# The start of a fused attention and two-MLP kernel: ramp and first tile written out as one list of operations and loads

## The chip, the cores and the metric

One core of a Trainium2 chip. The metric is the device time of one execution in microseconds, the median of three runs of the kernel.

## The reference, cut to what matters

```
# attention: q, k, v are (4 batches, 8 heads, 576, 64), f32
scores = q @ k^T / 8;  masked: heads 0-3 keep the last 32 keys,
                       heads 4-7 every 4th of the last 128 keys
attn = softmax(scores); x = attn @ v       # -> (2304 tokens, 512)
# first MLP:   h = x @ w_in (512 x 2048); x = (h * sigmoid(h)) @ w_out
# second MLP:  x = ((x @ w1) * (x @ w2)) @ w3 @ w_out2    -> (2304, 512)
```

## The kernel before

**Units of the attention.** A unit is three blocks of 64 queries of one pair of heads in one batch: 48 units, 12 for each batch. A unit goes through a chain of operations, each named by a letter that the schedule tables use. S: scores on TensorE (6 products of 64x96 into PSUM, L203, tiles `s`). M: mask, row maximum and copy to SBUF on VectorE (L218, tile `sm`). E: exponential and row sum on ScalarE (L228). N: sum to reciprocal on VectorE (L236, L238, tile `rs`), then the product with it on GpSimd (L239). T: transposition of the weights on TensorE (L246, tiles `t`). W: copy of it from PSUM to SBUF, tile `at`, on VectorE for batch 0 (L253) and on ScalarE after it (L255). V: product with the values on TensorE (L266, tiles `o`). O: the result in two parts into `xT`, high on ScalarE (L276), low on VectorE (L277).

**Precision by two parts.** Each f32 operand of the MLPs is split into a high part and a low part, and each product is three matmuls. The weights come from memory as 64-bit words and are converted by a chain in `Convert`: `rebias` on ScalarE (L398), `bits` in two passes on VectorE (L406, L408), `high` on ScalarE (L417), `low` on VectorE (L423). Four buffers (`rawp`) hold raw weights. The chain for w_in's block f is called i0, i1, ..., that for w_out's u0, u1, ...

**The first MLP** runs over five chunks of tokens (`CH1`: 512, 512, 256, 512, 512) and sixteen blocks f of hidden columns; one pair (chunk, block) is a slot. Slot (c, f) issues, in the order that a string in `SLOT` gives, the twelve matmuls of `h` for the next block (L686), the twelve matmuls of `x` for its own block (L720, tiles `x2`), the tanh of the next block (`t` in the string: L702 on ScalarE, L703 on VectorE), its split (`g`: L465 on ScalarE, L466 on VectorE), steps of the conversion (`m`, `c`) in chunk 0, and steps of the attention of later batches (`a`). The attention of batch b has to be in `xT` when a chunk wants its tokens.

**The ramp.** Before the first slot the twelve units of batch 0 have to be through. The kernel before makes it in rounds: round n issues the steps of the string `ATT0`, each operation with a lag (S0 of unit n, M1 of unit n-1, and so on), and takes units 12 and 13 along as far as T. Rounds 8 to 16 also take a micro-step of the conversion (`START`), and after rounds 14 and 15 the first nine matmuls of h for blocks 0 and 1 (`AHEAD`). Then come the rest of h for block 0, its tanh and split, and the slot (0, 0).

**Order and memory.** All instructions are issued in the order in which the program is written; each engine and each DMA queue takes its own in that order and waits for semaphores. Queries and keys of batch 0 lie in the first 1152 columns of `stage4` to `stage7`, its values in those of `stage0` to `stage3`; these tiles are 2048 columns wide and become the weight tiles wf8 to wf15 after the ramp. The attention's PSUM tiles of batch 0 come from `ps_x` (4 banks, S and T) and `ps_a` (2 banks, V). Every DMA of the inputs goes over SyncE's queue, except one of the first.

Of the kernel before, what the change touches and what calls it, by code (L numbers as in the profile page):

```python
# [68 lines left out]
def tile_kernel(  # L69
# [83 lines left out]
    def load_qk(i):  # L153
        if i < NPAIR:
            t = stage[NPAIR + i][:, :2 * S].rearrange("p (x s) -> p x s", x=2)
        else:
            t = qkp.tile([P, 2, S], F32, tag="qk", name=f"qk_{i}")
        qk[i] = t
        if i == 0:
            first = NB * QB  # L160
            nc.sync.dma_start(out=t[:, 0, :first], in_=qT_d[i][:, :first])
            nc.scalar.dma_start(out=t[:, 1, :first], in_=kT_d[i][:, :first])
            nc.sync.dma_start(out=t[:, 1, first:], in_=kT_d[i][:, first:])
            nc.sync.dma_start(out=t[:, 0, first:], in_=qT_d[i][:, first:])
        else:
            nc.sync.dma_start(out=t[:, 0], in_=qT_d[i])
            nc.sync.dma_start(out=t[:, 1], in_=kT_d[i])
# [23 lines left out]
    def a_scores(n):  # L191
        b, p, u = unit(n)
        t = qk[n // NU]
        if n < RAMP:
# [16 lines left out]
    def a_max(n):  # L211
# [3 lines left out]
        sm = smp.tile([P, NB, KB], F32, tag="sm", name=f"sm_{n}")  # L215
# [18 lines left out]
    def a_norm(n):  # L234
        sm, su = st[n]["sm"], st[n].pop("su")
        nc.vector.tensor_scalar_add(su[:, :NB], su[:, :NB], 1e-9)  # L236
        rs = stp.tile([P, 4, 1], F32, tag="rs", name=f"rs_{n}")
        nc.vector.reciprocal(rs[:, :NB, 0], su[:, :NB])  # L238
        nc.gpsimd.tensor_tensor(sm, sm, rs[:, :NB].to_broadcast([P, NB, KB]), op=ALU.mult)  # L239

# [8 lines left out]
    def a_evac(n):  # L249
        t_v = st[n].pop("t")  # L250
        at = atp.tile([KB, NB, P], F32, tag="at", name=f"at_{n}")
        if n < PER_B:
            nc.vector.tensor_copy(at, t_v)  # L253
        else:
            nc.scalar.activation(at, t_v, AF.Copy)  # L255
        st[n]["at"] = at
# [15 lines left out]
    def a_out(n):  # L272
        b, p, u = unit(n)
        o_v = st.pop(n)["o"]
        def put(dst, src):
            nc.scalar.activation(dst[:, 0], src, AF.Copy)  # L276
            nc.vector.tensor_sub(dst[:, 1], src, f32(dst[:, 0]))  # L277
# [38 lines left out]
    def attention_steps():  # L316

        steps, rounds, begun = [], [], {op: 0 for op in A_OPS}
        chain = "SMENTWVO"
        after = dict(zip(chain[1:], chain))  # L320
        ramp = [(n, ATT0, RAMP) for n in range(PER_B + 5)]
        for n, order, units in ramp + [(n, ATT, NUNIT) for n in range(RAMP, NUNIT + 4)]:
            for x in order.split("|"):
                step = []
                for op, lag in zip(x[::2], x[1::2]):
                    ready = begun[after[op]] if op in after else NUNIT
                    while begun[op] < min(n - int(lag) + 1, units, ready):
                        step.append((op, begun[op]))
                        begun[op] += 1
                if step:  # L330
                    steps.append(step)
                    rounds.append(n)
        return steps, rounds

    class Stream:
        def __init__(self):
            (self.steps, self.rounds), self.at, self.out = attention_steps(), 0, 0
# [33 lines left out]
    class Convert:  # L371


        def __init__(self):
            self.todo = []
            self.nb = self.nh = self.nl = 0
            self.gate = 1 << 30
# [22 lines left out]
        def bits(self, i, x):  # L400
# [6 lines left out]
            else:  # L407
# [4 lines left out]
                self.load(i + 2)  # L412
# [261 lines left out]
    hps, h_done, gt, xps = {}, {}, {}, {}  # L674

    def h_begin(c, f):
        if (c, f) not in hps:
            hps[c, f] = ps_h.tile([P, 512], F32, tag="h", name=f"h_{c}_{f}")
            h_done[c, f] = 0

    def h_kt(c, f, kt):
# [8 lines left out]
        h_done[c, f] += 1  # L690

    def h_part(c, f, half):
        h_begin(c, f)
        for kt in range(h_done[c, f], 2 * half + 2):
            h_kt(c, f, kt)

    def g_ops(c, f):

        n = CH1[c][1]
        ps = hps.pop((c, f))[:, :n]  # L700
        t = gp.tile([P, 512], F32, tag="t", name=f"t_{c}_{f}", bufs=1)[:, :n]
        nc.scalar.activation(t, ps, AF.Tanh, scale=0.5)  # L702
        nc.vector.scalar_tensor_tensor(t, t, 1.0, ps, op0=ALU.add, op1=ALU.mult)  # L703
        gt[c, f] = t

    def g_split(c, f):
        n = CH1[c][1]
        t = gt[c, f]
        g = gp.tile([P, 2, 512], F32R, tag="g", name=f"g_{c}_{f}")[:, :, :n]
        split(g, t)  # L710
        gt[c, f] = g

    def x2_part(c, f, half):
# [3 lines left out]
        g = gt[c, f] if half == 0 else gt.pop((c, f))  # L717
        todo = [(m, sa, 0) for m in range(KT) for sa in (0, 1)] + [(m, 0, 1) for m in range(KT)]
# [206 lines left out]
    with tc.manual_schedule():  # L925
        nc.vector.memset(mask, 0.0)
        for i in range(2):
            load_qk(i)
# [3 lines left out]
        load_v0(0)  # L932
        load_qk(2)
        cv.load(0)
        load_v0(1)
        load_qk(3)
        cv.load(1)
        load_v0(2)
        load_qk(NPAIR)
        load_v0(3)  # L940
        load_qk(NPAIR + 1)

        k = 0
        while att.out < PER_B:
            n = att.rounds[att.at]
            att.step()
            k += 1
            end = att.rounds[att.at] != n
            if (k == 4 and START.get(n, 0) > 1) or (end and n in START):
                cv.micro()  # L950
            if end:
                k = 0
                if n in AHEAD:
                    f = AHEAD[n]
                    cv.need(IN[f])
                    h_begin(0, f)
                    for kt in range(KT - 1):
                        h_kt(0, f, kt)
        assert att.out == PER_B
# [3 lines left out]
        h_part(0, 0, 1)  # L963
# [200 lines left out]
```

## Time and profile before

| | |
|---|---|
| median of 3 runs | 831.85 us (831.84 to 832.21) |
| the profiled execution's own time | 828.14 us |
| its span, first to last instruction | 826.4 us |
| TensorE matmuls busy | 806.7 us, 98% |
| VectorE, ScalarE, GpSimd busy | 483.1, 322.6, 56.4 us |
| chain that ended last, by engine | PE 79%, DVE 8%, ACT 5%, issue 3%, DMA 2%, POOL 1% |

The profiled execution is one of several, and its time lies 3.7 us under the median of the other runs; sums of durations are made against it. PE is TensorE, DVE VectorE, ACT ScalarE, POOL GpSimd, SP SyncE's queue. A busy TensorE is not a TensorE at its peak: ends of matmuls are modelled, and the distance from one start to the next says more. `s`, `t` and `o` rows of PE count two records for each product in part (x12 for six f32 products).

### The profile page before, as it was taken

Reading aid. Unit: us, or ns where it says so; the run is one execution under the profiler, and the core shown is the slowest. Engines: PE = TensorE matmul, PEld = TensorE weight load, DVE = VectorE, ACT = ScalarE, POOL = GpSimd, SP = SyncE. Lnnn points to the kernel's source line nnn. Section 1 sums busy time; section 2 is a strip of 40 time slices with the busy share of each in tenths; the row PEclk is TensorE's granted clock in tenths of the full one; section 3 lists DMA queues with packets and bytes.
Section 4 is the critical chain, followed back from the end, with each engine's and each line's share of the span. In section 5 each row is a group of like instructions: output and inputs, shape, how many; then the busy total and the mean of one; then the engine's idle time right before and its main releaser. Section 6 shows DMA issues by size and latency. Waiting matters only on the chain.

```text
span 826.4 us, 12870 instructions
## 1 busy us (share of the span) xinstructions
PE 806.7 (98%) x4848; PEld 686.2 (83%) x4848; DVE 483.1 (58%) x1179; ACT 322.6 (39%) x819; POOL 56.4 (7%) x90
## 2 busy tenths in 40 slices
PE   7889999999999999999999999999999999999997
PEld 5667777777788999888878887888889999999996
DVE  5877778333324443222358877768888554774544
ACT  5766766444324453222344545433423211221112
POOL 3201110000000110000000000012210000000000
PEclk9999999999999999999999999999999999999999
DMA  9855663211111202000087544535640752035202
GB/s 261 231 178 181 194 184 114 66 51 52 52 36 48 77 9 63 14 1 1 0 289 263 200 152 146 160 102 215 238 172 1 248 188 75 1 140 204 90 1 76
DMA packets 43454, 98.61 MB, mean 119 GB/s; under 512 B 3968, under 2 KB 21888, under 8 KB 41344
## 3 DMA queue, kind: packets, MB, share of 16 engines
q1 hardware_dynamic: 42784, 96.91, 35.6%
q10 hardware_dynamic: 608, 0.89, 0.4%
q8 instruction: 38, 0.62, 0.3%
q14 instruction: 24, 0.20, 0.1%
HBM read 73.66 MB, written 24.12 MB: 118 GB/s over the span
## 4 chain that ended last, share of the span: by engine, by line
PE 79%; DVE 8%; ACT 5%; issue 3%; DMA 2%; POOL 1%; SPq 0%; ACTq 0%; POOLq 0%; DVEq 0%
PE x L720 20%; PE h L686 19%; PE bank L840 19%; PE o L891 10%; PE wp L663 4%; PE o L266 2%; PE o L203 2%; ACT sm L228 2%; PE t L246 2%; DVE g L466 1%; DVE wf L423 1%; ACT raw_u L398 1%; DVE sm L218 1%; ACT t L702 1%; PE s L203 1%
## 5 line engine op out<-in xcount | busy, mean ns | idle before, releaser
L686 PE MATMUL h<-xT,wf 128*128 128x512 f32 (+1 forms) x960 | 220.2, 374 | 0.0
L720 PE MATMUL x<-g,wf 128*128 128x512 f32 (+1 forms) x960 | 215.7, 371 | 1.7 <-ACT g L465 1.7
L720 PEld LDWEIGHTS x<-g,wf 128*128 128x128 f32 x960 | 166.8, 188 | 33.0 <-ACT g L465 3.1
L686 PEld LDWEIGHTS h<-xT,wf 128*128 128x128 f32 x960 | 165.2, 188 | 32.0 <-ACT xT L276 0.2
L840 PE MATMUL bank<-xT,wf 128*128 128x384 f32 x864 | 164.5, 336 | 0.7 <-ACT s L858 0.4
L840 PEld LDWEIGHTS bank<-xT,wf 128*128 128x128 f32 x864 | 151.4, 188 | 9.0 <-ACT s L858 1.4
L703 DVE SCALAR_TENSOR_TENSOR t<-t,h 128x512 f32<-128x512 f32 (+1 forms) x80 | 50.6, 632 | 132.3 <-ACT t L702 132.2
L891 PE MATMUL o<-wf,wf 128*128 128x512 f32 x432 | 110.7, 393 | 0.0
L702 ACT ACTIVATE t<-h 128x512 f32<-128x512 f32 (+1 forms) x80 | 44.0, 551 | 120.2 <-PE h L686 118.8
L891 PEld LDWEIGHTS o<-wf,wf 128*128 128x128 f32 x432 | 80.1, 188 | 12.8
L466 DVE TENSOR_TENSOR g<-t,g 128x512 fp32r<-128x512 f32 (+1 forms) x80 | 58.1, 727 | 53.8 <-ACT g L465 53.0
L465 ACT ACTIVATE g<-t 128x512 fp32r<-128x512 f32 (+1 forms) x80 | 46.8, 585 | 43.5 <-DVE t L703 43.5
L876 ACT ACTIVATE wf<-c 128x384 fp32r<-128x384 f32 x48 | 25.2, 526 | 86.7 <-DVE c L874 86.5
L239 POOL TENSOR_TENSOR sm<-sm,rs 128x288 f32<-128x288 f32 x48 | 36.1, 752 | 267.5 <-DVE rs L238 212.2
L228 ACT ACTIVATE sm<-sm,nm 128x96 f32<-128x96 f32 x144 | 52.0, 367 | 5.6 <-DVE nm L218 5.6
L858 ACT ACTIVATE s<-bank 128x384 f32<-128x384 f32 x24 | 11.8, 490 | 95.3 <-PE bank L840 84.7
L663 PE MATMUL wp<-wf,wf 128*128 128x512 f32 x192 | 46.9, 392 | 0.3 <-DVE wf L579 0.3
L276 ACT ACTIVATE xT<-o 128x192 fp32r<-128x192 f32 (+6 forms) x58 | 17.6, 303 | 74.2 <-DVE nm L218 63.9
L663 PEld LDWEIGHTS wp<-wf,wf 128*128 128x128 f32 x192 | 35.7, 188 | 7.4 <-DVE wf L579 0.7
L865 DVE TENSOR_TENSOR c<-u,bank 128x384 f32<-128x384 f32 x36 | 19.9, 552 | 31.9 <-PE bank L840 31.7
L575 ACT ACTIVATE wf<-y 128x512 fp32r<-128x512 f32 (+1 forms) x40 | 22.7, 584 | 28.5 <-DVE y L536 13.5
L246 PE MATMUL t<-ident,sm 128*96 128x128 f32 x144 | 25.7, 289 | 6.0 <-POOL sm L239 6.0
(84 smaller groups left out, 764.0 us busy)
## 6 DMA issues: line engine op xcount, KB each, us to landing
rawj<-in_w_dram SPq DMA_DIRECT2D x32, 512.0 KB, 3.8
raw_i<-in_w_in_dram SPq DMA_DIRECT2D x16, 512.0 KB, 3.9
raw_u<-in_w_out_dram SPq DMA_DIRECT2D x16, 512.0 KB, 3.5
setd<-wf SPq DMA_DIRECT2D x8, 1024.0 KB, 3.9
wf<-setd SPq DMA_DIRECT2D x8, 1024.0 KB, 5.2
setd<-wf SPq DMA_DIRECT2D x8, 768.0 KB, 5.8
wf<-setd SPq DMA_DIRECT2D x8, 768.0 KB, 6.8
xb<-x2d SPq DMA_DIRECT2D x12, 384.0 KB, 7.9
```

Of the source, the lines that this page charges most:

```text
L228: nc.scalar.activation(sm[:, j], sm[:, j], AF.Exp, bias=nm[:, j:j + 1], scale=-1.0, accum_out=su[:, j:j + 1],)
L239: nc.gpsimd.tensor_tensor(sm, sm, rs[:, :NB].to_broadcast([P, NB, KB]), op=ALU.mult)
L246: nc.tensor.transpose(t_ps[:KB, j], sm[:, j], ident)
L465: nc.scalar.activation(dst[:, 0], src, AF.Copy)
L466: nc.vector.tensor_sub(dst[:, 1], src, f32(dst[:, 0]))
L663: nc.tensor.matmul(wp_ps[i], a[:, i // 2, sa, i % 2 * P:(i % 2 + 1) * P], o[:, sb], start=(jt == 0 and x == 0), stop=(jt == NG - 1 and x = ...
L686: nc.tensor.matmul(ps, win(f, sa, kt), xT[:, kt, sb, r0:r0 + n], start=(kt == 0 and x == 0), stop=(kt == KT - 1 and x == 2),)
L702: nc.scalar.activation(t, ps, AF.Tanh, scale=0.5)
L703: nc.vector.scalar_tensor_tensor(t, t, 1.0, ps, op0=ALU.add, op1=ALU.mult)
L720: nc.tensor.matmul(xps[c][m][:, :n], wout(f, sa, m), g[:, sb], start=(f == 0 and sa == 0 and sb == 0), stop=(f == NF - 1 and sb == 1),)
L840: nc.tensor.matmul(b, a_op(s, a, sa, kt), b_op(x, sb, kt), start=(n == 0), stop=(n == 5),)
L891: nc.tensor.matmul(ops[pr][m], g_block(jj, n, sa)[:, m % 3 * P:(m % 3 + 1) * P], wp_v(f, sb), start=(first_ and x == 0), stop=(last and x ...
```

## The change

The ramp's rounds, `START`'s micro-steps, `AHEAD` and the first slot are replaced by one string, `START`, which lists every operation with its unit, and `FIRST`, which lists the loads in order. The letters are those above, with four splits: N becomes R (sum and reciprocal, VectorE) and N (product, GpSimd); O becomes H (high) and L (low); the copy after T is W (VectorE) or X (ScalarE), chosen for each unit; r, a, b, h, l are the conversion's five passes, p the matmuls of h by quarters, t u g e the tanh, its product, high and low split, x00 and x01 the halves of the first slot's `x`. Units 12 and 13 are no longer in it: the attention of batch 1 starts in slot (0, 1) with S of unit 12. Units 0 to 11 keep `sm` in columns 1152 to 1439 and `at` in columns 1440 to 1823 of the stage tile n mod 8, instead of in pools of three and two buffers. Queries and keys of units 12 to 17 are loaded inside the list (d4, d5). Raw weights are loaded four ahead, as soon as a buffer is free, instead of two ahead.

```
-ATT0 = "N3|W4|M1|V5S0L4|T3|E2|O5"
-RAMP = PER_B + 2
+START = (
+    "S0 M0 E0 S1 M1 E1 S2 R0 M2 N0 E2 R1 S3 N1 M3 S4 E3 R2 M4 T0 N2 S5 X0 R3 T1 "
...
+    "L6 W9 V8 H7 b0 T10 H8 X10 R11 h0 L7 N11 L8 V9 r1 l0 V10 H9 a1 T11 H10 L9 p00 X11 L10 "
...
+)
+FIRST = "q0a k0a k0b q0b q1 k1 v0 k2 q2 v1 i0 k3 q3 v2 i1 v3 u0 i2"
 ATT = "V3S1L3|M1T2O3|W2E1|N1"
-START = {8: 1, 9: 1, 10: 1, 11: 2, 12: 2, 13: 2, 14: 2, 15: 2, 16: 1}
-AHEAD = {14: 0, 15: 1}
...
-        sm = smp.tile([P, NB, KB], F32, tag="sm", name=f"sm_{n}")
+        if n < PER_B:
+
+            o = NU * NB * P
+            sm = stage[n % 8][:, o:o + NB * KB].rearrange("p (j k) -> p j k", j=NB)
+        else:
+            sm = smp.tile([P, NB, KB], F32, tag="sm", name=f"sm_{n}")
...
-    def a_evac(n):
+    def a_evac(n, act=True):
         t_v = st[n].pop("t")
-        at = atp.tile([KB, NB, P], F32, tag="at", name=f"at_{n}")
         if n < PER_B:
+            o = NU * NB * P + NB * KB
+            at = stage[n % 8][:KB, o:o + NB * P].rearrange("p (j k) -> p j k", j=NB)
+        else:
+            at = atp.tile([KB, NB, P], F32, tag="at", name=f"at_{n}")
+        if act:
+            nc.scalar.activation(at, t_v, AF.Copy)
+        else:
             nc.vector.tensor_copy(at, t_v)
...
-                self.load(i + 2)
+                self.load(self.ahead)
+                self.ahead += 1
...
+        BEGIN = {
+            "S": a_scores, "M": a_max, "E": a_exp, "R": a_sum, "N": a_mul, "T": a_transpose,
+            "W": lambda n: a_evac(n, False), "X": a_evac, "V": a_av, "H": a_high, "L": a_low,
+            "r": cv.rebias, "a": lambda i: cv.bits(i, 0), "b": lambda i: cv.bits(i, 1),
+            "h": cv.high, "l": cv.low, "d": load_qk, "t": lambda f: g_tanh(0, f), "u": lambda f: g_mul(0, f),
+            "g": lambda f: g_high(0, f), "e": lambda f: g_low(0, f),
+        }
+        for z in START.split():
+            op, z = z[0], z[1:]
+            if op == "p":
+                h_first(z)
+            elif op == "x":
+                x2_part(0, int(z[0]), int(z[1]))
+            else:
+                BEGIN[op](int(z))
+            if op == "b":
+                cv.nb = cv.nh = cv.nl = int(z) + 1
+        for n in range(PER_B - 3, PER_B):
+            a_loads(n)
...
-        for i, (c, f) in enumerate(slots):
+        for i, (c, f) in list(enumerate(slots))[1:]:
```

What moves on the engines is shown at three places. First TensorE at the end of the ramp. A name such as t_10 carries the unit, h_0_1 the chunk and the block; the last number is a counter. Before, from unit 11's transposition on:

```order
L246 MATMUL t_11_647<-ident_113,sm_11_552 96x128 x3
L686 MATMUL h_0_0_663<-xT_112,wf0_96 128x512 x9
L266 MATMUL o_10_679<-at_10_630,stage3_107 64x64 x6
L246 MATMUL t_12_688<-ident_113,sm_12_592 96x128 x3
L686 MATMUL h_0_1_706<-xT_112,wf1_97 128x512 x9
L266 MATMUL o_11_722<-at_11_677,stage3_107 64x64 x6
L246 MATMUL t_13_732<-ident_113,sm_13_632 96x128 x3
L686 MATMUL h_0_0_663<-xT_112,wf0_96 128x512 x3
L266 MATMUL o_12_763<-at_12_720,v_12_611 64x64 x6
L203 MATMUL o_12_763<-qk_4_200 64x96 x6
L686 MATMUL h_0_1_706<-xT_112,wf1_97 128x512 x3
```

Now, from unit 10's transposition on:

```order
L272 MATMUL t_10_564<-ident_113,stage2_106 96x128 x3
L296 MATMUL o_9_577<-stage1_105,stage3_107 64x64 x6
L296 MATMUL o_10_586<-stage2_106,stage3_107 64x64 x6
L272 MATMUL t_11_596<-ident_113,stage3_107 96x128 x3
L723 MATMUL h_0_0_602<-xT_112,wf0_96 128x512 x3
L296 MATMUL o_11_615<-stage3_107 64x64 x6
L723 MATMUL h_0_0_602<-xT_112,wf0_96 128x512 x9
L723 MATMUL h_0_1_649<-xT_112,wf1_97 128x512 x12
```

The work of units 12 to 14 has left this stretch (the first slot's twelve `x` matmuls follow in both, and then, now, S of unit 12 and h of block 2), and the matmuls of h for blocks 0 and 1 stand together behind unit 11. Of the ramp's first part TensorE's order differs less: the first twelve steps are in both S of units 0 to 6, T of units 0 to 2 and V of units 0 and 1; S of unit 4 now stands ahead of T of unit 0, and S of unit 5 ahead of T of unit 1.

Second, VectorE in the list's second half, where the conversion's passes stand among the last units (L308 is L, L285 W, L254 and L256 R, L444, L446 and L462 a, b and l):

```order
L285 COPY stage1_105<-t_9_547 96x384
L446 SCALAR_TENSOR_TENSOR y_i0_540<-raw_i0_192,y_i0_540 128x512
L254 TENSOR_SCALAR su_11_543<-su_11_543 128x3
L256 RECIPROCAL rs_11_571<-su_11_543 128x3
L308 TENSOR_TENSOR xT_112<-o_7_532,xT_112 128x192
L308 TENSOR_TENSOR xT_112<-o_8_553,xT_112 128x192
L462 TENSOR_TENSOR wf0_96<-y_i0_540,wf0_96 128x512
L444 TENSOR_SCALAR y_i1_594<-raw_i1_198 128x512
L308 TENSOR_TENSOR xT_112<-o_9_577,xT_112 128x192
L308 TENSOR_TENSOR xT_112<-o_10_586,xT_112 128x192
L446 SCALAR_TENSOR_TENSOR y_i1_594<-raw_i1_198,y_i1_594 128x512
L444 TENSOR_SCALAR y_u0_626<-raw_u0_202 128x512
```

The chain of i0 now ends behind unit 11's reciprocal, and those of i1, u0 and i2 lie behind it; before, the passes of i0 stood between the units' operations from 22.4 us (L406) to 30.8 us (L423). Copies of all twelve units' transposed weights stood on VectorE before; six of them are now on ScalarE.

Third, SyncE's queue of loads behind the ramp's own, now:

```order
L425 DMA raw_u0_202<-in_w_out_dram 128x1024
L425 DMA raw_i2_204<-in_w_in_dram 128x1024
L425 DMA raw_u1_562<-in_w_out_dram 128x1024
L425 DMA raw_i3_610<-in_w_in_dram 128x1024
L166 DMA qk_4_612<-in_qT_dram 128x576
L166 DMA qk_4_612<-in_kT_dram 128x576
L425 DMA raw_u2_634<-in_w_out_dram 128x1024
L166 DMA qk_5_636<-in_qT_dram 128x576
```

Queries and keys of unit 12 (`qk_4`) stood before ahead of the values in `stage3` and of u0; now they stand behind the load of i3, which waits for a raw buffer to be free.

## Rows read from the trace of the kernel before

**Rows 1.** The page's first line.

```profile
span 826.4 us, 12870 instructions
```

**Rows 2.** Busy us by stretch: length, then PE, PEld, DVE, ACT, POOL; clock; DMA.

```profile
17.26:33.00 15.74, 12.81 (x210) 9.71 (x208) 14.62 (x85) 14.01 (x62) 5.34 (x8) 1.00 1.10 270
33.00:47.81 14.81, 13.45 (x116) 9.60 (x114) 10.45 (x29) 8.06 (x24) 2.06 (x2) 1.00 0.59 182
56.40:132.04 75.64, 73.95 (x512) 55.72 (x510) 60.46 (x172) 49.44 (x141) 9.34 (x10) 1.00 0.58 182
132.04:148.90 16.86, 16.86 (x77) 13.89 (x76) 12.82 (x30) 9.26 (x21) 0.93 (x1) 1.00 0.17 59
```

**Rows 3.** Timeline of PE, 9 to 19 us: start, us, instruction, count.

```profile
9.74 0.87 PE L246 MATMUL t<-ident,sm 128*96 128x128 f32 x3
10.54 1.23 PE L203 MATMUL s<-stage 64*64 64x96 f32 x12
11.70 0.87 PE L246 MATMUL t<-ident,sm 128*96 128x128 f32 x3
...
16.14 1.19 PE L203 MATMUL s<-stage 64*64 64x96 f32 x12
17.26 0.53 PE L246 MATMUL t<-ident,sm 128*96 128x128 f32 x3
17.72 0.57 PE L266 MATMUL o<-at,stage 96*64 96x64 f32 x12
18.22 0.71 PE L203 MATMUL s<-stage 64*64 64x96 f32 x12
18.86 0.54 PE L246 MATMUL t<-ident,sm 128*96 128x128 f32 x3
```

**Rows 4.** Waits of PE, 0 to 48 us: total, times, longest.

```profile
PE t L246 <- POOL sm L239: 3.1, 5, 1.1
```

**Rows 5.** Timeline of PE, second slot and the start of the third; [idle before <-releaser].

```profile
46.67 0.57 PE L266 MATMUL o<-at,v 96*64 96x64 f32 x12 [0.71 <-DVE y_i L408]
...
47.81 1.66 PE L686 MATMUL h<-xT,wf 128*128 128x512 f32 x6
...
56.40 1.67 PE L686 MATMUL h<-xT,wf 128*128 128x512 f32 x6
```

**Rows 6.** Timeline of DVE, one whole unit of the attention, 19.9 to 21.5 us.

```profile
19.91 0.24 DVE L218 CUSTOM_DVE_ANT_0 sm<-s,mask 128x96 f32<-128x96 f32 x1
...
20.44 0.35 DVE L277 TENSOR_TENSOR xT<-o,xT 128x192 fp32r<-128x192 f32 x1
20.71 0.15 DVE L236 TENSOR_SCALAR su<-su 128x3 f32<-128x3 f32 x1
...
21.04 0.55 DVE L253 COPY at<-t 96x384 f32<-96x384 f32 x1
21.51 0.24 DVE L218 CUSTOM_DVE_ANT_0 sm<-s,mask 128x96 f32<-128x96 f32 x1
```

**Rows 7.** Timeline of DVE, 28 to 29 us, weight conversion.

```profile
28.07 0.42 DVE L406 TENSOR_SCALAR y_i<-raw_i 128x512 int32<-128x512 int32 x1
28.41 0.35 DVE L277 TENSOR_TENSOR xT<-o,xT 128x192 fp32r<-128x192 f32 x1
28.67 0.68 DVE L408 SCALAR_TENSOR_TENSOR y_i<-raw_i,y_i 128x512 int32<-128x512 int32 x1
29.27 0.16 DVE L236 TENSOR_SCALAR su<-su 128x3 f32<-128x3 f32 x1
```

**Rows 8.** Line L239, 0 to 60 us: count, ns least/median/most.

```profile
L239 POOL TENSOR_TENSOR sm<-sm,rs x16: 666/667/1397, 8.1 to 57.2; 128x288 f32<-128x288 f32 x16
```

**Rows 9.** Line L466, 40 to 130 us: ns least/median/most.

```profile
L466 DVE TENSOR_TENSOR g<-t,g x12: 693/1155/1156, 42.9 to 125.7; 128x512 fp32r<-128x512 f32 x12
```

**Rows 10.** Chain that ended last: start, us, what.

```profile
135.10 2.72 PE x L720 x12
```

**Rows 11.** DMA issues, 35 to 48 us: KB each, us to landing.

```profile
qk<-in_kT_dram SPq DMA_DIRECT2D x1, 288.0 KB, 4.8
```

More of the change, by code (lines that the diff above doesn't have):

```diff
@@ L158, in load_qk, with load_part @@
         qk[i] = t
[L159 to L164, printed above, removed]
-        else:
-            nc.sync.dma_start(out=t[:, 0], in_=qT_d[i])
-            nc.sync.dma_start(out=t[:, 1], in_=kT_d[i])
+        for x in (0, 1) if i >= NPAIR else ():
+            nc.sync.dma_start(out=t[:, x], in_=(qT_d, kT_d)[x][i])
+    def load_part(what):
+        i, part, first = int(what[1]), what[2:], NB * QB
+        if what[0] in "qk":
+            x, r = "qk".index(what[0]), {"a": slice(0, first), "b": slice(first, S), "": slice(0, S)}[part]
+            if i not in qk:
+                load_qk(i)
+            queue = nc.scalar if what == "k0a" else nc.sync
+            queue.dma_start(out=qk[i][:, x, r], in_=(qT_d, kT_d)[x][i][:, r])
+        elif what[0] == "v":
+            load_v0(i)
+        else:
+            cv.load((IN if what[0] == "i" else OUT)[i])
     def blocks(i, j, n_):
@@ L232, in a_exp, with a_sum @@
         st[n]["su"] = su
[L234 to L235 removed]
+    def a_sum(n):
+        su = st[n].pop("su")
         nc.vector.tensor_scalar_add(su[:, :NB], su[:, :NB], 1e-9)
@@ L316, in attention_steps @@
     def attention_steps():
-        steps, rounds, begun = [], [], {op: 0 for op in A_OPS}
+        steps, begun = [], {op: PER_B for op in A_OPS}
         chain = "SMENTWVO"
         after = dict(zip(chain[1:], chain))
-        ramp = [(n, ATT0, RAMP) for n in range(PER_B + 5)]
-        for n, order, units in ramp + [(n, ATT, NUNIT) for n in range(RAMP, NUNIT + 4)]:
-            for x in order.split("|"):
+        for n in range(PER_B, NUNIT + 4):
+            for x in ATT.split("|"):
                 step = []
@@ L376, in __init__ @@
             self.nb = self.nh = self.nl = 0
+            self.ahead = 4
             self.gate = 1 << 30
@@ L926, in tile_kernel @@
         nc.vector.memset(mask, 0.0)
-        for i in range(2):
-            load_qk(i)
+        first_loads = FIRST.split()
+        for x in first_loads[:6]:
+            load_part(x)
         build_masks(False)
@@ L931, in tile_kernel, with h_first @@
         build_masks(True)
[L932 to L959, printed above, removed]
+        for x in first_loads[6:]:
+            load_part(x)
+        def h_first(z):
+            f, kt = int(z[0]), int(z[1])
+            if kt == 0:
+                h_begin(0, f)
+            h_kt(0, f, kt)
+        BEGIN = {
[17 more added lines that the diff above has]
+            a_loads(n)
         wf[NF // 2:] = [weights_tile(i) for i in range(NF // 2, NF)]
         slots = [(c, f) for c in range(NC1) for f in range(NF)]
-        h_part(0, 0, 1)
-        cv.need(OUT[0])
-        g_ops(0, 0)
-        g_split(0, 0)
         begin = [lambda i=i: x_sum(i) for i in range(2)]
```

67 lines of the change are left out of this document (41 added, 26 removed), and 5 rows, old and new, of the table START.

## The prediction

> **What bounds the kernel now.** I start from the span, 826.4 us [rows 1], against the profiled execution's own time of 828.14 us: 1.7 us lie around the span and don't change here. TensorE is busy nearly all of it, so the question is where its starts lie further apart than its work. Busy time by stretch shows it: from 17.26 to 33.00 us TensorE is busy 12.81 of 15.74 us while VectorE is busy 14.62, and from 33.00 to 47.81 us 13.45 of 14.81; in the slots that follow, from 56.40 to 132.04 us, 73.95 of 75.64 [rows 2]. What the change can win lies ahead of 56 us.
>
> The timeline of TensorE gives the price of its work there, as the distance from one start to the next. Until 17.26 us one S takes 1.16 us (10.54 to 11.70) and one T 0.80; from 17.26 us on T takes 0.46, V 0.50, S 0.64 [rows 3]. The granted clock in the rows is 1.00 throughout, yet the durations change as between the two levels of 1.2 and 2.4 GHz, after a stretch from 9.74 us on in which each step starts where the one before it has streamed. Twelve f32 matmuls with 512 columns take 2.72 us [rows 10].
>
> **Work against time before.** I count from 17.26 us to the start of h for block 2, the beginning of the second slot's matmuls, at 47.81 us [rows 5]: 30.55 us. In it lie 9 S, 11 T, 12 V (the attention up to unit 15's scores) and h0, h1 and the first `x`, by the order of the instructions: 9 x 0.64 + 11 x 0.465 + 12 x 0.50 + 3 x 2.72 = 25.0 us. So 5.5 us are lost. The waits of TensorE name 3.1 us of them as five waits of a T for GpSimd's product [rows 4], which starts late because VectorE is full; 0.71 us more is the wait at 46.67 us [rows 5]. VectorE's timeline says why: one unit takes 1.60 us there (19.91 to 21.51): M 0.53, L 0.27, R 0.33, W 0.47 [rows 6], as long as TensorE's 0.64 + 0.46 + 0.50, and the conversion's passes come on top.
>
> **The change, part by part.** *Up to 17.26 us: nothing.* TensorE's first twelve steps are the same set, the first six loads keep their order, and the low level binds. I take the same time at which the level changes.
>
> *The floor behind it.* TensorE now has 6 S (unit 12's with them), 9 T, 10 V, h0, h1 and `x` up to h of block 2: 3.84 + 4.19 + 5.00 + 8.16 = 21.2 us, so T2, the start of h of block 2, is 38.5 us at the earliest.
>
> *VectorE's floor.* It starts M of unit 6 when S of unit 6 has ended, at about 17.4 us. Up to the pass l of u0, which the first `x` needs, it has 6 M, 7 R, 11 L, 5 W [rows 6], four a at 0.34, four b at 0.60 (28.67 to 29.27), three l like b, and the product u of the tanh like b [rows 7]: 3.2 + 2.3 + 3.0 + 2.4 + 1.4 + 4.2 + 0.6 = 17.0 us, so 34.4 us. TensorE gets to that `x` at 38.5 - 0.64 - 2.72 = 35.1 us. VectorE is 0.7 us ahead; four of the six copies that went to ScalarE lie in this stretch, and with them it would be 1.2 us behind. ScalarE was busy 14.01 of 15.74 us before [rows 2]; it loses the exponentials of units 12 and 13 and gets the copies, so I let it bind nowhere but in the order of its steps.
>
> *Waits that stay.* I walk the list by these durations, engine by engine, and add what an instruction waits for. Three places hold TensorE. V of unit 5: its W stands on VectorE behind W of unit 4, M of unit 8, R of unit 7 and L of unit 3, starts at 21.7 us and takes 0.55; TensorE is there at 21.95 and waits 0.4 us. V of unit 7: its W waits on VectorE behind R of unit 9, which waits for ScalarE's exponential, and TensorE loses 0.3 us. T of unit 11: R of unit 11 stands behind W of unit 9 and b of i0 and starts at 28.6 us; GpSimd's 0.67 us [rows 8] follow, T starts near 29.9, and the first h, behind l of i0, at 30.3, 0.4 us more than the two waits before explain. Sum 1.1 us; T2 = 39.6 us.
>
> *GpSimd beside VectorE.* The split of g (L466), with two inputs in SBUF, takes 0.69 us at best and 1.16 us in most slots [rows 9], where GpSimd's product starts just ahead of it; that product takes 1.40 us once against 0.67 [rows 8]. In the list only N of unit 11 meets such a pass, l of i0, and it gates the first h: I add 0.46 us. T2 = 40.1 us. Nearest rows bound it between 0 and 0.46 for each of seven such passes (four b, three l), 3.2 us.
>
> The Trainium skill (SBUF — State Buffer, "Who interferes with whom") says that a VectorE instruction with two SBUF inputs and a GpSimd instruction that reads SBUF exclude each other, the later one blocking for the whole of the other. The rows agree that they collide. By that rule, if N of units 9, 10 and 11 each met such a pass, 3 x 0.67 us would be lost in place of 0.46, and T2 would be 41.7 us, an estimate.
>
> *The debt.* What left the ramp comes back in the slots. Before, ten slots with one unit each run from 56.40 to 132.04 us, 7.56 us a slot [rows 2, 5], then three without attention, and h of block 0 of the next chunk starts at 148.90. Now slot (0, 1) has only S of unit 13 besides h and `x`: 2 x 2.72 + 0.64 = 6.1 us. Slots (0, 2) to (0, 14), thirteen, have a whole unit each, in the same order of instructions: 98.3 us. So that h starts at T2 + 104.4. There the old kernel is one T ahead (0.4 us), and from the third chunk on both are in the same place in order. Shift: T2 + 104.4 + 0.4 - 148.9 = T2 - 44.1 us. For T2 = 40.1 us: **4.0 us earlier**.
>
> *Loads and memory at nothing.* Units in stage columns and raw weights four ahead cost no instruction; queries and keys of units 12 to 17 leave the first stretch of loads, so the values and u0 land earlier than TensorE or ScalarE want them. That cover is gone for one load, below.
>
> Span 822.4 us, own time 824.1; on the runs' median 831.85 - 4.0 = **827.9 us**.
>
> **Rivals.** *TensorE alone (faster still).* If the waits vanish and the collision too, T2 = 38.5 and the shift is -5.6 us: 826.2 us. For it: each wait is a few tenths, and the list was laid to meet. Against: VectorE has only 0.7 us of room, and its waits are of a chain.
>
> *Unit 12's keys late.* On SyncE's queue qk_4 stands behind i3, which waits for b of i1 on VectorE, about 31.7 us by the walk. The same pair landed 4.8 us after its issue behind one raw load [rows 11], so here at 37 to 38 us. S of unit 12 stands on TensorE ahead of h of block 2 and is reached at 39.5 us. Behind it everything waits. With 2 us more it lands at about 40 us and costs 0.5; with 4 us, 2.5 us: 830.4 us at worst; middle 829.4 us.
>
> *VectorE binds the ramp's end.* If all seven two-input passes collide, VectorE is 3.2 us later, less the 0.46 counted: T2 = 42.9, shift -1.2 us, 830.6 us. The change would then not do what it says, but fill one engine as full as before. Against: b at 28.67 us takes 0.68 us [rows 7], no longer than its work, while GpSimd has a product in each unit's 1.6 us.
>
> *The clock rises late (slower).* TensorE at the low level needs 1.16 for 0.64 [rows 3], so each microsecond more of it loses 0.45. The order up to 17.26 us has only small changes, but a T or V that waits there could open gaps. The walk's own waits of about 1.6 us would hide behind slower matmuls. If the level rose only behind unit 11's V, the 12.3 us of S, T and V would take 22.2, 9.9 us more, less 1.6: T2 = 48.4, shift +4.3 us, 836.2 us. It decides from T2 = 44.1 on, a rise some 12 us late, about 30 us. Against: between 9.74 and 17.26 us all inputs of the new order are there by the walk.
>
> **How the numbers follow.** Chances: forecast 0.65, TensorE alone 0.12, late keys 0.09, VectorE 0.09, clock 0.05. 0.2% (1.7 us) is about what a measurement of this kernel can tell. The first three are faster by over that, 0.86; VectorE's case is within it, 0.09; the clock's is slower, 0.05. The range goes from TensorE alone, less 0.4 us for slots that start with room, to VectorE's case: 825.8 to 830.6 us; outside lie the clock and the edges of the others. The likeliest alone: 826.8 to 829.0.
>
> **What would show it.** Right: the level changes at 17 to 18 us; V of unit 11 starts at about 31 us; `x` of block 0 at 36 us; h of block 2 at 40 us; slots (0, 2) to (0, 14) 7.56 us apart; from the third chunk on all starts about 4 us earlier. Wrong: S or T at the low level's durations past 18 us; an S of unit 12 that waits for a load; slots longer than 7.56 us, each tenth of which costs 1.3 us over thirteen; or a wait in the third chunk for attention that came late.

## The result and the profile after

The changed kernel takes 818.92 us (818.67 to 819.25, four runs) against 831.95 us of the kernel before in the same session (831.84 to 832.21, four runs): ratio 0.9843, interval 0.9826 to 0.986, 13.0 us faster. Its profiled execution took 818.67 us. The forecast was 827.9 us and a range of 825.8 to 830.6: the sign was right and the size was not. The kernel before was timed again beside every group of experiments; its median there lay between 829.7 and 831.2 us, its single runs between 827.3 and 833.9, while the changed kernel stayed within 817.8 to 819.9.

The first line of the page:

```profile
span 816.9 us, 12913 instructions
```

Busy time by stretch (columns as in [rows 2]), the end of the ramp in two parts and chunk 0's slots in two:

```profile
13.36:28.82 15.46, 13.24 (x233) 10.34 (x232) 12.51 (x70) 13.42 (x59) 5.35 (x8) 1.00 0.86 222
28.82:38.90 10.08, 10.08 (x65) 7.85 (x63) 9.82 (x20) 8.16 (x17) 0.00 (x0) 1.00 0.77 256
53.41:89.38 35.97, 35.97 (x257) 28.16 (x255) 28.34 (x82) 23.82 (x69) 3.76 (x4) 1.00 0.62 193
89.38:142.31 52.93, 51.78 (x359) 38.99 (x357) 41.73 (x120) 33.36 (x96) 6.58 (x8) 1.00 0.43 140
```

TensorE now loses 2.2 us up to T of unit 11 and nothing from there to h of block 2, where before [rows 2] it lost 2.9 and 1.4 us in two stretches of 15 us. Timeline of TensorE, from the rise of the level to h of block 2:

```profile
11.40 1.23 PE L216 MATMUL s<-stage 64*64 64x96 f32 x12
12.56 0.87 PE L272 MATMUL t<-ident,stage 128*96 128x128 f32 x3
13.36 0.59 PE L296 MATMUL o<-stage 96*64 96x64 f32 x12
13.88 0.53 PE L272 MATMUL t<-ident,stage 128*96 128x128 f32 x3
...
20.92 0.57 PE L296 MATMUL o<-stage,stage 96*64 96x64 f32 x12 [0.56 <-DVE stage L285]
...
24.99 0.57 PE L296 MATMUL o<-stage,stage 96*64 96x64 f32 x12 [0.58 <-DVE stage L285]
...
27.95 0.92 PE L296 MATMUL o<-stage,stage 96*64 96x64 f32 x24 [0.68 <-PE t L272]
...
30.06 0.57 PE L296 MATMUL o<-stage 96*64 96x64 f32 x12
...
35.45 2.88 PE L763 MATMUL x<-g,wf 128*128 128x512 f32 x12
38.26 0.71 PE L216 MATMUL s<-qk 64*64 64x96 f32 x12
38.90 3.02 PE L723 MATMUL h<-xT,wf 128*128 128x512 f32 x12
```

The level rises at 13.4 us, not at 17.26 [rows 3]: T goes from 0.80 to 0.46 us from start to start. V of unit 11 starts at 30.06 us (forecast 31), `x` of block 0 at 35.45 (36), h of block 2 at 38.90 (40.1; before 47.81 [rows 5]). Waits of TensorE up to 54 us:

```profile
PE o L296 <- DVE stage L285: 1.3, 3, 0.6
...
PE h L723 <- DVE wf L462: 0.8, 1, 0.8
PE o L296 <- PE t L272: 0.7, 1, 0.7
```

The five waits for GpSimd of [rows 4] are gone. The wait of 0.68 us is that of V of unit 9. In the slots that follow, h starts at these times (timeline of TensorE, three of its rows):

```profile
53.41 1.68 PE L723 MATMUL h<-xT,wf 128*128 128x512 f32 x6
...
89.38 1.67 PE L723 MATMUL h<-xT,wf 128*128 128x512 f32 x6
...
96.95 1.67 PE L723 MATMUL h<-xT,wf 128*128 128x512 f32 x6
```

Five slots from 53.41 to 89.38 are 7.20 us long, TensorE without a gap; from 89.38 on they take 7.57, as most of them did before [rows 2, 5]. In chunk 1 a slot takes 7.07 us against 7.21 before, by the order on TensorE: T now stands next to V and S, before between two halves of `x`. The changed kernel's timeline there:

```profile
157.21 0.57 PE L296 MATMUL o<-at,v 96*64 96x64 f32 x12
157.71 0.71 PE L216 MATMUL o<-qk 64*64 64x96 f32 x12
158.35 0.53 PE L272 MATMUL t<-ident,sm 128*96 128x128 f32 x3
158.64 1.64 PE L723 MATMUL h<-xT,wf 128*128 128x512 f32 x6
```

**Where 13.0 us are.** Of the two profiled executions, own times 828.14 and 818.67 us, the starts of h give: 8.9 us by h of block 2; 6.6 left at the first h of chunk 1 (142.31 against 148.90), so the slots give back 2.3; 7.2 at the first h of chunk 2 (250.04 against 257.22); 9.4 at the end, 1.9 of the last 2.2 in the last chunk of the first MLP and 0.3 in the second MLP. The other 3.6 us are not in this pair: the profile of before lay 3.7 us under its timed runs.

### The profile page after: what moved, and what is told of

Same layout as the page of the kernel before. It is cut to its first block, busy times and chain, and to the rows that moved or that the text cites. A ratio compares the mean times of both kernels' runs of the same rounds, so it can differ in the third digit from the quotient of the medians.

```text
span 816.9 us, 12913 instructions
## 1 busy us (share of the span) xinstructions
PE 801.7 (98%) x4848; PEld 685.4 (84%) x4848; DVE 482.4 (59%) x1173; ACT 323.9 (40%) x825; POOL 61.6 (8%) x90
## 4 chain that ended last, share of the span: by engine, by line
PE 80%; DVE 8%; ACT 5%; issue 3%; DMA 1%; POOL 1%; SPq 0%; ACTq 0%; DVEq 0%; POOLq 0%
PE h L723 20%; PE x L763 20%; PE bank L883 20%; PE o L934 11%; PE wp L702 4%; PE o L296 2%; PE o L216 2%; PE t L272 2%; ACT sm L246 1%; DVE g L751 1%; DVE wf L462 1%; ACT t L737 1%; ACT raw_i L436 1%; DMA stage<-in_kT_dram 1%; DVE y_i L444 1%
## 5 line engine op out<-in xcount | busy, mean ns | idle before, releaser
L763 PE MATMUL x<-g,wf 128*128 128x512 f32 (+1 forms) x960 | 211.7, 369 | 0.0
L261 POOL TENSOR_TENSOR sm<-sm,rs 128x288 f32<-128x288 f32 x36 | 33.4, 928 | 240.0 <-DVE rs L256 139.7
L246 ACT ACTIVATE sm<-sm,nm 128x96 f32<-128x96 f32 x108 | 39.0, 367 | 0.0
L908 DVE TENSOR_TENSOR c<-u,bank 128x384 f32<-128x384 f32 x36 | 19.9, 552 | 31.9 <-PE bank L883 31.7
L236 DVE CUSTOM_DVE_ANT_0 sm<-o,mask 128x96 f32<-128x96 f32 x102 | 20.7, 251 | 22.4 <-PE o L216 22.1
```

The costliest lines, as they stand in the source:

```text
L246: nc.scalar.activation(sm[:, j], sm[:, j], AF.Exp, bias=nm[:, j:j + 1], scale=-1.0, accum_out=su[:, j:j + 1],)
L763: nc.tensor.matmul(xps[c][m][:, :n], wout(f, sa, m), g[:, sb], start=(f == 0 and sa == 0 and sb == 0), stop=(f == NF - 1 and sb == 1),)
```

## The experiments

The theory after the result: the ramp, held by single late steps, pays most, and the list gains by never letting TensorE wait long. Rivals are named with each run. Times are medians; the kernel before that was run beside them took 830.08, 831.17, 830.40 and 829.69 us in the four groups.

**The two kernels again.**

> The kernel before, unchanged, profiled once more. Theory: its first profiled execution (828.14 us) was 3.7 us shorter than its other executions by the landing of loads; this one takes 831 to 833 us, and TensorE waits about 5 us instead of 1.2 us for the split behind the raw weights at the start of the last chunk, with h of block 2 still at 47.8 us. Rival: TensorE's level rises later in the usual execution, S at 1.16 us beyond 17.3 us and h of block 2 at 51 to 52 us.

> The changed kernel, unchanged, profiled once more. Theory: as in its first profile, 818.5 to 819.3 us, the level rises at 13 to 14 us, h of block 2 starts at 38.9 us, the first six whole slots of the first chunk take 7.20 us and the others 7.56. Rival: the level's rise is a matter of the execution and falls anywhere from 13 to 18 us, with h of block 2 between 38.9 and 40.5 us.

Measured: 829.85 us (827.56 to 833.24, ratio 0.9999, interval 0.998 to 1.0017) and 819.46 (817.79 to 819.87, ratio 0.9862, 0.9835 to 0.989). Both theories fell in part. The kernel before ran no slower than its other executions, had no wait at the start of the last chunk, and h of block 2 came later, not at 47.8 us. In the changed kernel the level rose earlier than either text allowed: T takes 0.46 us from start to start at 8.90 us already, h of block 2 starts at 37.7 us, and five slots, not six, take 7.20 us. The second profile of the kernel before shows in the ramp what the first did not. Waits of ScalarE, and of TensorE:

```profile
ACT raw_u L398 <- DMA raw_u<-in_w_out_dram: 3.1, 1, 3.1
```

```profile
PE t L246 <- POOL sm L239: 6.6, 5, 3.6
```

and its busy time by stretch (columns as in [rows 2]; the clock is the third figure from the right):

```profile
25.00:30.00 5.00, 4.24 (x69) 3.17 (x69) 3.77 (x22) 1.38 (x6) 1.33 (x2) 1.00 1.04 324
30.00:35.00 5.00, 1.39 (x8) 1.21 (x6) 3.39 (x14) 4.94 (x23) 0.67 (x1) 0.87 1.10 260
35.00:40.00 5.00, 5.00 (x29) 3.83 (x29) 2.58 (x8) 1.60 (x4) 1.40 (x1) 0.79 0.48 154
```

The raw load of u0 comes 3.1 us after ScalarE wants it. The exponential of a unit is queued behind it, the sum, GpSimd's product and a T behind that; T waits 3.6 us, and TensorE then works in part at the level of 1.2 GHz. h of block 2 starts at 50.1 us, 2.3 later than in the first profile, where the same load was 0.4 us late. The DMA engines are full (share 1.04 to 1.10) up to 35 us. From this pair of profiles h of block 2 is 12.4 us earlier with the change, where the first pair gave 8.9.

The changed kernel's second profile, of its fastest run, has a stretch at 1.2 GHz too. Busy time by stretch, and TensorE at its start, the same two V as at 27.95 us in the first profile:

```profile
25.34:28.75 3.41, 3.38 (x30) 2.70 (x30) 2.69 (x6) 2.61 (x6) 0.67 (x1) 0.50 0.45 159
```

```profile
25.37 1.55 PE L296 MATMUL o<-stage,stage 96*64 96x64 f32 x24 [0.68 <-PE t L272]
```

The waits of 0.56, 0.58, 0.22 and 0.68 us ahead of it stand at the same steps in the first profile, where the granted clock stayed at 1.00. From V of unit 9 to V of unit 11 it took 3.50 us here and 2.11 there, so this stretch cost 1.4 us.

**Units 12 and 13 out of the ramp.**

```diff
-RAMP = PER_B + 2
+RAMP = PER_B
```

> The kernel before with one part of the change alone: units 12 and 13 leave the ramp's rounds (RAMP = 12), the rounds, pools and loads are as before. Theory (the debt is neutral, as the prediction's sum has it): h of block 2 starts 3 to 3.5 us earlier, about 44.5 us, and the thirteen whole slots at 7.56 us give it back: 831.5 to 832.5 us. Rival: slots that begin with room take 7.20 us for a while, and the part alone wins 2 us or more: 829.5 to 830 us.

Measured: 830.7 us (827.9 to 833.52), ratio 1.0008 (0.9988 to 1.0028). Alone it is worth nothing, as the theory had it, though not by the theory's steps: in this profile (833.28 us, one of the slowest two of ten runs) u0 was 5.5 us late in the ramp, a T waited 5.8 us, and h of block 2 started later than before, not earlier.

**u0 and i2 loaded ahead of the later keys; only the last keys behind them; both edits together.**

```diff
         load_v0(2)
-        load_qk(NPAIR)
         load_v0(3)
+        cv.load(2)
+        cv.load(3)
+        load_qk(NPAIR)
         load_qk(NPAIR + 1)
```

> The kernel before with one change: the raw loads of u0 and i2 are issued ahead of the queries and keys of units 12 to 17. Theory (u0's raw load, queued behind 1.15 MB of queries and keys, holds ScalarE and so TensorE's transpositions, 0.4 us in the first profile and 3.1 and 5.5 us in the later ones): the wait of ScalarE for raw_u is gone, the longest wait of a T for GpSimd is about 1.2 us, and the time is about 3 us less, 826.5 to 828.5, with a narrower spread, unless S of unit 12 now waits for its keys. Rival (the wait is filled by other work, or it was chance of the later profiles): 829.5 to 832, no different from the kernel before.

In the next one `load_qk(NPAIR)` keeps its place, and the two `cv.load` lines stand ahead of `load_qk(NPAIR + 1)`.

> The kernel before with one edit: the queries and keys of units 15 to 17 alone (0.58 MB) are loaded behind u0 and i2; those of unit 12 keep their place. Theory (the loads arrive one behind the other at some 270 KB per us, and u0 is the late one): u0 lands about 2 us earlier, nobody in the ramp wants what went behind it, and the time is 1.5 to 3 us under the kernel before. Rival (what the ramp gains there it waits for elsewhere, as with both edits before): within 1 us of it.

The third has the diff above and `RAMP = PER_B`.

> The kernel before with two edits together: units 12 and 13 are out of the ramp, and the raw loads of u0 and i2 stand ahead of the queries and keys of units 12 to 17. Each edit alone changed nothing. Theory (the ramp's loads arrive one behind the other and are full up to some 33 us; with one edit alone either u0 or the keys of unit 12 is still wanted before it can have landed; with both nobody wants the last 1.15 MB early): TensorE's wait of 3.6 to 5.8 us is gone, h of block 2 starts at 45 to 47 us instead of 50 to 52, and the time is 3 to 5 us under the kernel before. Rival (those waits hide others of the old order): within 1 us of the kernel before.

Measured: 830.07 us (ratio 0.9994, 0.9975 to 1.0013), 829.93 (0.9991, 0.9973 to 1.0009) and 828.06 (0.9973, 0.9957 to 0.999). My theory fell for the first two. With u0 ahead, TensorE waits for the keys of unit 12 instead, which the old order wants at 26 us:

```profile
PE s L203 <- DMA qk<-in_kT_dram: 4.7, 1, 4.7
```

and with the last keys alone moved, u0 still landed 3.6 us late and a T waited 4.3 us: the values in `stage3` and u0 arrived no earlier in that execution. Only when nobody wants the keys early are 2.3 us won, less than the theory's 3 to 5, and this profile still has a V that waits 1.4 us for values and a granted clock of 0.50 from 22.8 to 33.0 us. So late loads are a part of what the old ramp loses, not the larger one, and neither of the two orders of them alone cures it.

**All parts but the list.** The kernel of the third run above, with the code that puts `sm` and `at` of units 0 to 11 in the stage tiles.

> The kernel before with all parts of the change but the list: units 12 and 13 out of the ramp, u0 and i2 loaded ahead of the later keys, and the scores and transposed weights of batch 0 in the stage tiles' unused columns; the rounds and lags of the old order stay. Theory (storage pays by letting work run ahead, which only the list's order makes use of): within 1.5 us of the kernel with the first two edits alone, some 5 to 8 us above the changed kernel. Rival (storage pays by itself, since the pools of two and three buffers held VectorE and ScalarE back in the old order too): 4 to 6 us under it, close to the changed kernel.

Measured: 829.11 us (825.84 to 832.25), ratio 0.9988 (0.9969 to 1.0006), 1.0 us above the kernel without the storage. The theory held: the storage is worth nothing in the old order. The list, with the copies on ScalarE that are part of it, brings the remaining 10 us (829.11 against 818.9 and 819.5).

**The list without the storage, and each half of it.** In the first, both tiles come from the pools of three and two buffers again; in the second `sm` alone, in the third `at` alone:

```diff
-        if n < PER_B:
-            o = NU * NB * P
-            sm = stage[n % 8][:, o:o + NB * KB].rearrange("p (j k) -> p j k", j=NB)
-        else:
-            sm = smp.tile([P, NB, KB], F32, tag="sm", name=f"sm_{n}")
+        sm = smp.tile([P, NB, KB], F32, tag="sm", name=f"sm_{n}")
```

> The changed kernel with the scores and the transposed weights of batch 0 in the old pools of three and two buffers instead of columns of the stage tiles, list and loads as changed. Theory (the storage carries the list): M of unit 3 waits for T of unit 0, and so on, since the list issues M three and more units ahead of T; h of block 2 starts 2 to 4 us later than 38.9, 821 to 823 us. Rival (the order alone does it): within 0.5 us of the changed kernel, 818.5 to 819.5 us.

> The changed kernel with the scores of batch 0 back in their pool of three buffers; the transposed weights stay in the stage tiles. Theory (the pool of two buffers for the transposed weights carries the storage's 6 us, since the copy of a unit waits for the product of the unit two before it): within 1.5 us of the changed kernel. Rival (the scores carry it: the row maximum of a unit waits for the transposition of the unit three before, and the list runs S far ahead): 4 to 7 us more, 823 to 826, with gaps on TensorE that keep it at the low level past 20 us.

> The changed kernel with the transposed weights of batch 0 back in their pool of two buffers; the scores stay in the stage tiles. Theory (they carry the storage's 6 us): 4 to 7 us more than the changed kernel, 823 to 826, with waits of a V for its copy of over 1 us. Rival (the scores carry it): within 1.5 us of the changed kernel.

Measured: 825.65 us (823.09 to 829.7, ratio 0.9932, 0.9904 to 0.996), 823.52 (822.96 to 826.59, 0.9935, 0.9914 to 0.9955) and 819.4 (817.1 to 821.0, 0.9881, 0.9857 to 0.9905). The scores carry it, which was the rival; the place of the transposed weights makes no difference that shows. Waits of the kernel with `sm` in its pool, 12 to 34 us:

```profile
DVE sm L231 <- PE t L267: 5.7, 4, 3.5
PE o L291 <- DVE stage L280: 4.9, 4, 1.5
```

The row maximum of a unit needs the buffer of the unit three before it, and VectorE stands still until that one's T is through; the copies queued behind it come late, and V waits. Its timeline of TensorE:

```profile
14.37 0.88 PE L267 MATMUL t<-ident,sm 128*96 128x128 f32 x3
16.54 0.91 PE L291 MATMUL o<-stage,stage 96*64 96x64 f32 x12 [1.29 <-DVE stage L280]
17.38 2.19 PE L216 MATMUL s<-stage 64*64 64x96 f32 x24
19.49 0.87 PE L267 MATMUL t<-ident,sm 128*96 128x128 f32 x3
...
21.52 0.53 PE L267 MATMUL t<-ident,sm 128*96 128x128 f32 x3
```

T still takes 0.87 us at 19.5 us, and the level rises at about 21 us, 7 later than in the changed kernel's first profile. That is the prediction's clock rival at work, in a kernel where it can be seen; but this profile is of the slowest of six runs, 826.59 us, and how late the level rose in the others is not on record.

**All copies of transposed weights on VectorE.** In the list, X0, X2, X6, X8, X10 and X11 become W.

> The changed kernel with one part undone: the six copies of transposed weights that went to ScalarE are on VectorE again. Theory of the prediction (VectorE has 0.7 us of room; with the four copies back that lie behind 17 us it is 1.2 us behind): the first x and h of block 2 start 1 to 2.5 us later, time 819 to 821. Rival (ScalarE's queue is as full, so the copies' place makes no difference): within 0.5 us of the changed kernel.

Measured: 823.64 us (819.89 to 824.41), ratio 0.9918 (0.9894 to 0.9941): 4 to 5 us more than the changed kernel. The direction is the theory's; the size is about twice as large. Its timeline of TensorE, and its busy time by stretch:

```profile
27.49 1.55 PE L296 MATMUL o<-stage,stage 96*64 96x64 f32 x24 [1.29 <-issue]
28.98 0.88 PE L272 MATMUL t<-ident,stage 128*96 128x128 f32 x3
29.50 1.63 PE L723 MATMUL h<-xT,wf 128*128 128x512 f32 x3
```

```profile
23.00:28.00 5.00, 2.77 (x48) 2.02 (x44) 4.63 (x15) 3.62 (x15) 1.75 (x3) 0.90 0.60 190
28.00:33.00 5.00, 5.00 (x41) 3.81 (x39) 3.70 (x9) 2.19 (x6) 0.78 (x1) 0.50 0.28 95
```

VectorE is busy 4.63 of 5 us, a V waits 1.29 us, and behind it TensorE works at a granted clock of 0.50: two V take 1.55 us where the changed kernel's take 0.92. The changed kernel shows the same 1.55 us in its second profile, behind a shorter wait and for half as long: the stretch at 0.50 lasts 6.8 us here. This profile is of a run of 821.64 us, the second fastest of six; h of block 2 starts at 41.1 us in it. What its slower runs lose besides was not seen.

**Loads of the changed kernel.**

```diff
-FIRST = "... q2 v1 i0 k3 q3 v2 i1 v3 u0 i2"
+FIRST = "... q2 v1 i0 k3 q3 v2 i1 d4 v3 d5 u0 i2"
```

(with d4 and d5 taken out of `START`)

> The changed kernel with one part undone: queries and keys of units 12 to 17 are loaded again ahead of the values of the last units and of u0. Theory (part of the gain is u0's raw load coming in time): ScalarE waits 2 to 5 us for raw_u, the first x starts later, and the time is 1 to 4 us more, 820.5 to 823.5, with a wider spread. Rival (the new order of operations has room for a late u0): within 1 us of the changed kernel.

```diff
-                self.load(self.ahead)
-                self.ahead += 1
+                self.load(i + 2)
```

> The changed kernel with one part undone: raw weights are loaded two blocks ahead again, not four. Theory (four ahead is worth nothing, since a raw block lands in about 5 us and two blocks ahead are a whole slot): within 1 us of 819. Rival (the slots of 7.20 us at the start of chunk 0 come from raw weights that are there earlier): these slots become 7.56 us, six of them, and the time is 2.2 us more, 821.

Measured: 817.28 us (816.72 to 818.94, ratio 0.984, 0.982 to 0.9861) and 817.78 (816.45 to 819.15, 0.9843, 0.9821 to 0.9866). Neither is slower than the changed kernel. With the old order of loads u0 landed at 27.7 us in the profile and ScalarE took it at 28.4, so the first theory fell: the new order of operations asks for it no earlier. Four blocks ahead or two is the same.

**Why slots of 7.57 us.** In chunk 0's string of steps:

```diff
-    "ahmamHxaXmtmmacg",
+    "ahammHxaXmtmmacg",
```

> The changed kernel with one change in chunk 0's slots: one step of the weight conversion (0.68 us on VectorE) stands behind the attention's row maximum instead of ahead of it; TensorE's order is the same. Theory (the last seven slots of chunk 0 take 7.57 us instead of 7.20 because a loop of VectorE and ScalarE, row maximum, high part of the output, exponentials, tanh, split, conversion pass, is longer than TensorE's work): the pass leaves that loop, all slots take about 7.2 us, and the time is 2.6 us less, about 816.5. Rival (the 7.57 us are TensorE's own work beside GpSimd's product): no slot changes, within 0.5 us of 819.

Measured: 815.79 us (814.28 to 816.84), ratio 0.9818 (0.9797 to 0.9839). In its profile the slots from 96 us on start like this:

```profile
95.80 1.68 PE L723 MATMUL h<-xT,wf 128*128 128x512 f32 x6
...
103.00 1.67 PE L723 MATMUL h<-xT,wf 128*128 128x512 f32 x6
...
131.78 1.68 PE L723 MATMUL h<-xT,wf 128*128 128x512 f32 x6
```

All are 7.20 us. The same place in the changed kernel, VectorE's timeline, shows the loop that the pass `low` (L462) left:

```profile
98.12 1.16 DVE L751 TENSOR_TENSOR g<-t,g 128x512 fp32r<-128x512 f32 x1
99.20 0.68 DVE L462 TENSOR_TENSOR wf<-y_u,wf 128x512 fp32r<-128x512 f32 x1
99.80 0.24 DVE L236 CUSTOM_DVE_ANT_0 sm<-o,mask 128x96 f32<-128x96 f32 x1
...
100.86 0.36 DVE L308 TENSOR_TENSOR xT<-o,xT 128x192 fp32r<-128x192 f32 x1 [0.46 <-ACT xT L315]
...
103.86 0.69 DVE L741 SCALAR_TENSOR_TENSOR t<-t,h 128x512 f32<-128x512 f32 x1 [0.98 <-ACT t L737]
```

The row maximum stands behind `low`, ScalarE's high part and exponentials behind the row maximum, the tanh behind them, and the next product and split behind the tanh. Once the head start that the ramp leaves is used up, this loop of 7.57 us sets the pace and not TensorE's 7.20.

**A kernel that beats both.** The edit above, and eight short products of zeros on TensorE ahead of S of units 0, 1 and 3:

```diff
+WARM = {"0": 5, "1": 2, "3": 1}
...
+                nc.tensor.matmul(warm_ps[:, :448], warm[:, :P], warm, start=True, stop=True)
```

> The changed kernel with two edits: the conversion's step behind the row maximum in chunk 0's slots, which gave 2.6 us by the slots, and eight short products of zeros on TensorE in its idle time of the first microseconds. Theory (TensorE's level rises at 9 to 14 us, as chance has it, and each microsecond at the low level loses up to 0.45): the level rises by 9 us, h of block 2 starts at 37 to 38 us in every execution, time about 814.5 to 815.5. Rival (early steps wait for loads anyway, or the products delay the first scores): no better than the first edit alone, 815.8 or more.

Measured: 814.45 us (813.32 to 819.29), ratio 0.9828 (0.9799 to 0.9857). Its profile has the high level from the first T on (0.46 us from start to start at 10.03), and h of block 2 at 37.4 us. Against the edit of the slots alone, 815.79 us, it is not told apart: one of its six runs is the slowest of both kernels. "In every execution" fell: two runs, 817.07 and 819.29 us, show a mean granted clock of 0.998 and 0.993, so part of them was at the low level all the same. Most of the 4.5 us under the changed kernel is the slots'.

## Why the prediction came out as it did

Of the 9.0 us between the forecast of 4.0 and the 13.0 measured, 1.2 lie in the ramp, 2.0 in the slots behind it, 2.2 far behind the change, and 3.6 in the execution against which the sum was made.

**The sign and the ramp: right, and the waits mostly where they were put.** V of unit 5 waited 0.56 us (0.4 forecast), V of unit 7 0.58 (0.3); the third place lay just ahead of T of unit 11, which had been named: V of unit 9, with 0.68 us (0.4). S of unit 12 started at 38.26 us without a wait, 0.3 us behind its keys, which landed at 38.0 us as the rival had put it. The estimate of VectorE's room missed a copy: five of the six that went to ScalarE (X2, X6, X8, X10, X11) lie behind M of unit 6, not four, so with them it would be 1.65 us behind by the same sum and not 1.2.

**"Up to 17.26 us: nothing" failed, by 1.9 us.** The level rose at 13.4 us, and TensorE was through its first twelve steps at 15.4 us, not 17.26; it then waited 2.2 us where 1.6 had been put, so that 1.2 us are left at h of block 2. In the other profiles of kernels that time like the changed one the rise lies between 8 and 14 us, and h of block 2 starts at 37.7 to 39.2. In the other six profiles of kernels with rounds it lies between 9 and 14 us as well, so the 1.9 us are the chance of the two executions and not the change's work. A moment that one execution shows was taken for a property of the kernel. The clock rival's own price was 0.8 us too high: at the low level its S, T and V take 1.16, 0.80 and 0.84 us, 21.4 us in all and not 22.2.

**"GpSimd beside VectorE": too dear.** Only `low` of i0 met the product of unit 11, as forecast; it took 0.96 us, against 0.68 alone. No instruction of TensorE waited for it, so the 0.46 us were not lost. The Trainium skill (SBUF — State Buffer, "Who interferes with whom") has the later of the two blocked for the whole of the other. The trace agrees that the two collide, but at 0.28 us here beside a product of 0.67 us: `low` started 0.42 us before the product's end, so by that rule it would have taken 1.10 us, an estimate from these spans. The prediction's 41.7 us by the rule stood for three such meetings; one took place.

**"The debt" failed, by 2.0 us.** Thirteen slots were put at 7.56 us; one took 8.19, with the wait of 0.8 us for `wf` in it, five 7.20, and seven 7.57. The price had been read from slots which the VectorE loop already bound; that a kernel with a head start runs at TensorE's own pace first was given 0.4 us, and only at the edge of the range, where it was worth 1.8. From h of block 2 to the first h of chunk 1 it took 103.4 us where 104.4 had been put. The 0.4 us for a T in chunk 1 became a gain of 0.6, since slots there are 0.14 us shorter.

**"What the change can win lies ahead of 56 us" failed, by 2.2 us.** The last chunk of the first MLP, where 1.9 of them lie, has the same instructions in the same order. One slot of it took 6.98 us before and 5.44 after. Ahead of it stands the store of the chunk before, whose issue to landing took, in the two profiles:

```profile
x2d<-x2s SPq DMA_DIRECT2D x2, 512.0 KB, 5.1
```

```profile
x2d<-x2s SPq DMA_DIRECT2D x2, 512.0 KB, 3.5
```

Weights that reuse its buffers are loaded behind it, and ScalarE waited 4.3 us for them before, 2.8 after, with the tanh behind it. The store's time is no chance: it took 4.2 to 5.1 us in all seven profiles of kernels with rounds and 3.2 to 3.6 in all ten with the list. What TensorE loses by it is partly chance: its wait there was 1.25 us in this profile, and at most 0.87 us in the other six with rounds, none in one. Why the store lands earlier stays open.

**"What bounds the kernel now" failed by 3.6 us.** The sum was made against one profile, 3.7 us under the median; the text said so and carried the difference over unchanged. But the executions of the old ramp differ in the very part that the change removes: h of block 2 at 47.8 us with u0 0.4 us late, at 50.1 with u0 3.1 late. The part of 13.0 us that is gained in a usual execution is therefore larger than in that one. How late u0 was in each timed run, no profile shows, but the granted clock of most is on record. Up to its last matmul the profiled execution has no stretch at 0.50 behind the first rise; its mean is 1.00. Of 87 later runs of this kernel 75 show a mean of 0.996 or less, most of them 0.995. Of 827 us, 0.005 less than 1.00 is some 8 us at 0.50, up to 2 of them behind the last matmul. At the price in the changed kernel, 1.4 us lost in 3.4, that makes 2.5 to 3 us, an estimate. It is not the whole: the medians go from 829.0 us (12 runs at 0.997 or more) to 831.7 (7 at 0.993 or less), but one run at 0.999 took 831.84.

**What makes up the list's 10 us.** Out of the runs: the scores' storage is worth 4 to 6 us with the list and nothing without it; the copies on ScalarE 4 to 5 us; units 12 and 13 with their loads 2.3 us in the old order. These overlap and are not to be added. In the profiles of the kernels that lack one of them and time slower, TensorE waits 1.1 to 5.8 us at a time in the ramp; in the changed kernel's two profiles no wait behind 13 us is longer than 0.8 us. A granted clock of 0.50 goes with it, but does not set the two apart: such a stretch, of 3.4 to 17 us, lies in all but one of the slower kernels' profiles, the first of the kernel before, and also in the changed kernel's second, a run of 817.79 us. How much of the 10 us is the waits' length and how much the level was not separated. The prediction had a low level as a rival for the kernel after, with a chance of 0.05. It should have asked whether the usual execution of the kernel before was in it.

## What to carry to other kernels

Before a stage's gain is summed from one profile, compare that execution's own time with the timed runs: where it is several microseconds faster, look for the load, the wait or the clock in the changed stage that was lucky, by a second profile and by the granted clock of the timed runs, and price it at its usual value. Price moved work by the engine that would bind it where it goes, with the head start that it arrives with, not by the mean of a stretch that another engine already held. Here buffers that let one engine run ahead paid only with an order that uses them.

## What the runs showed of the hardware that was not expected

TensorE's level can fall without a long wait, and with the same waits it can hold: in the changed kernel's second profile the granted clock was 0.50 for 3.4 us behind waits of at most 0.68 us, and two V took 1.55 us instead of 0.92; in the first, with the same waits, it stayed at 1.00. What decides is not shown. Up to the rise of the level the clock in the rows is 1.00 although the durations are those of the low level (T 0.80 us from start to start, 0.46 later), so the durations tell more there. And the same sequence of loads lands at different speeds: u0 was issued at 18.9, 20.7 and 21.7 us and came at 28.3, 29.6 and 31.4 us in three profiles with one order of loads, while the DMA engines were full in each (share 1.10 to 1.11 from 15 to 28 us).
